# A packed V for quad 3, its transposes inside the next K, and four masks on GpSimd

## The chip, the cores and the metric

The kernel runs on one core of one Trainium2 chip. The metric is the device time of one execution in microseconds (us). Before the change it is 3111.47 us, the median of 3 runs (3111.46 to 3111.81).

## What is computed

A sequence of 2048 positions with 640 channels goes through four layers, A, B, A, B, each behind a layer norm and added to its input. Layer A cuts the sequence into 64 segments of 32 positions. Each segment is put behind 8 memory rows, so that 40 rows attend to each other in 32 heads of 192 channels, and its first 8 output rows are the memory of the next segment. Layer B is a sliding window: each position attends to 8 positions at a distance of 0, 2, ... 14, in 32 heads of 20 channels.

```python
# layer A, one segment: h = [mem; xs], 8 + 32 rows
scores = jnp.einsum('bhqe,bhke->bhqk', q, k) * scale
scores = jnp.where(mask[None, None], scores, -1000000000.0)
p = _softmax(scores, axis=-1)
o = jnp.einsum('bhqk,bhke->bhqe', p, v)
o = jnp.einsum('bhte,hed->btd', o, Wo)
mem = o[:, :M, :].copy()
...
x = x + _A_ref(_layernorm(x, axis=-1), A_mem0, A_Wq, A_Wk, A_Wv, A_Wo, A_seg_len)
x = x + _B_ref(_layernorm(x, axis=-1), B_wqkv, B_wo)
x = x + _A_ref(_layernorm(x, axis=-1), A_mem0, A_Wq, A_Wk, A_Wv, A_Wo, A_seg_len)
x = x + _B_ref(_layernorm(x, axis=-1), B_wqkv, B_wo)
```

## The kernel before, in words

**Lanes and steps.** The two A layers share their weights, and so do the two B layers. The kernel therefore works on two segments at once, called lanes: lane 0 is segment t of the first pair of layers, lane 1 is segment t - 2 of the second pair. A step t does layer A for both lanes (80 columns, NT, of 2 x 40 rows) and, threaded through it, layer B of the step before (64 columns). There are 66 such steps and a last one for layer B alone; 62 of the 66 have both lanes. `one_lane()` is true in the first two and the last two, and what is said below of packing holds for the 62 others.

**Quads.** The 32 heads of layer A are worked in 8 quads of four, numbered 0 to 7. For quad i TensorE computes K (`a_k`), Q (`a_q`) and V (`a_v`), 30 matmuls of 80 columns each, by `proj` (L286); then the scores (`a_s`, 8 matmuls), and, one quad later, the product of probabilities and V (`a_pv`, 8 matmuls). The output projection (`a_o`) of quad i - 5 is put between. The order on every engine is the order in which the program issues the instructions: `run` (L974) puts TensorE, ScalarE, VectorE, GpSimd and SyncE under a manual schedule. `step` (L865) writes that order out by hand. For quad i it is: K of i; the transposes of V of quad i - 1, if that is not packed; Q of i; a piece of layer B (`b_first`); `a_pv` of quad i - 1; V of i; another piece of layer B (`b_second`); the normalisation of quad i - 1 (`a_norm`); the scores of i and their exponential; the mask.

**V and its transposes.** V comes out of TensorE with its channels on the partitions; `a_pv` needs the keys there. `a_v` (L336) copies it to SBUF (tile vT), TensorE transposes it into PSUM (tile ps_vt), and copies bring it into the tile Vt. Without packing (`a_vt`, L354) there are 6 transposes of 128 columns and one VectorE copy (L363). With packing (`a_vt_packed`, `a_vt_main`, `a_vt_rest`), quads 1, 5 and 6 so far, the 80 key rows of two head pairs are laid into 4 transposes: 64 rows of one head pair and the other's fill the 128 rows of three of them, and the 16 left of each share the fourth. That fourth one is copied to the tile Vx (L372) and from there into Vt with six small copies (L387 to L389, three for each head pair), and VectorE copies the rest in two pieces (L380). In quads 5 and 6 GpSimd makes three of the small copies and ScalarE the other three.

**Softmax.** ScalarE makes E, the exponential of the scores (L403). The mask is a product of E with zeros and ones (`a_mask`, L410 for a packed quad, L413 for the others), on VectorE but for quad 5, where GpSimd makes it. The sum over keys comes from columns of ones in Vt. After `a_pv`, ScalarE turns the sums into reciprocals (tile R: four logarithms, L429, and one exponential, L431), and VectorE multiplies (`a_norm`, L439 to L441).

**Layer B.** Its pieces lie at: quad 1, its Q and K; quads 1 to 3, the expansion of its queries on GpSimd (`b_qexp`, L607, five of them, tile QX with two buffers); quads 2 and 3, its scores in four groups (`b_s`, L622, groups 0 and 2 ahead of `a_pv`, 1 and 3 behind `a_s`), their exponentials on ScalarE (tile EB, L628) and masks on VectorE (`b_mask`, L635); quad 3, five transposes of its V (`b_vt`, L596) and two copies of them (tile VB, L600); quad 5, its products (`b_pv`).

The weights come by DMA from the SyncE queue. `used` frees a slot of the weight ring and `prefetch` issues the next load.

Of the kernel before, what the change touches and what calls it, by code (L numbers as in the profile page):

```python
# [13 lines left out]
ALU = mybir.AluOpType  # L14
# [3 lines left out]
P = 128  # L18
# [8 lines left out]
NT = 2 * LT  # L27
# [7 lines left out]
BG = 8  # L35
# [11 lines left out]
MM = 5  # L47
VH = 512
PK = P - NT
PACKED = (1, 5, 6)  # L50

def half_order():

# [27 lines left out]
class Kernel:  # L81
# [201 lines left out]

        return self.acc[int(c >= 3)], c - 3 * int(c >= 3)

    def proj(self, kind, i, t):  # L286

        nc = self.nc
        hT = self.hT
        ps = self.big(f"ps_{kind}", {"k": 0, "q": 1, "v": 2}[kind])  # L290
        w = [self.units[kind, i, h] for h in range(2)]
        mem_last = kind == "k" and i == 0
        order = [(n, c) for c in range(NC) for n in range(6)] if mem_last else [(n, c) for n in range(6) for c in range(NC)]
        for n, c in order:
            if n == 3 and c == 0 and not mem_last:
                self.used(kind, i, (0,))
            nc.tensor.matmul(ps[:, NT * n + self.c0:NT * n + self.c1], lhsT=w[n // 3][:, c, P * (n % 3):P * (n % 3 + 1)],  # L297
                             rhs=hT[:, NT * c + self.c0:NT * c + self.c1],
                             start=(c == 0 and (n == 0 or not mem_last)), stop=(c == NC - 1), skip_group_check=mem_last)
        self.used(kind, i, (0, 1) if mem_last else (1,))  # L300
        return ps

    def a_k(self, i, t):
        nc = self.nc
        ps = self.proj("k", i, t)
        pv = self.cols(ps[:, 0:6 * NT].rearrange("p (a b n) -> p a b n", a=2, b=3))
        h4 = lambda tl: self.cols(tl[:, 0:4 * NT].rearrange("p (a j n) -> p a j n", a=2, j=2))
        kf, kz = h4(self.KF), h4(self.Kz)
        nc.scalar.copy(out=kf, in_=pv[:, :, 0:3:2, :])  # L309
        nc.scalar.copy(out=kz[0:64, :, 0, :], in_=pv[0:64, :, 1, :])  # L310
        nc.scalar.copy(out=kz[64:P, :, 1, :], in_=pv[64:P, :, 1, :])
# [38 lines left out]
    def packed(self, i):  # L350

        return i in PACKED and not self.one_lane()

# [21 lines left out]
    def a_vt_main(self):  # L375
# [3 lines left out]
        for a in range(2):  # L379
            self.nc.vector.tensor_copy(out=dst[64 * a:64 * (a + 1), a], in_=src[64 * a:64 * (a + 1)])  # L380

    def a_vt_rest(self, a, copy):

        halves = lambda v: v.rearrange("p (b c) -> p b c", b=2)
        r0, n = ((64, 16), (32, 32))[a]
        row = self.Vt[r0:r0 + n, VH * a:VH * (a + 1)]
        copy(out=row[:, 0:128], in_=self.Vx[0:n])  # L387
        copy(out=halves(row[:, 128:384])[:, :, 0:64], in_=halves(self.Vx[32:32 + n]))
        copy(out=row[:, 320:448], in_=self.Vx[64:64 + n])  # L389
# [13 lines left out]
        nc.scalar.activation(out=self.cols(e[0:self.rows]), in_=self.cols(sv[0:self.rows]), func=ACT.Exp, scale=float(DH) ** -0.5)  # L403
        self.em = e

    def a_mask(self, eng=None):
        nc, e = self.nc, self.em
        n = self.c1 - self.c0
        if self.rows == P:
            (eng or nc.vector).tensor_tensor(out=e[:].rearrange("p (a j) n -> p a j n", a=2), in0=e[:].rearrange("p (a j) n -> p a j n", a=2),  # L410
                                    in1=self.maskA[:].unsqueeze(2).to_broadcast([P, 2, 2, NT]), op=ALU.mult)
            return
        nc.vector.tensor_tensor(out=self.cols(e[0:NT]), in0=self.cols(e[0:NT]),  # L413
                                in1=self.cols(self.maskA[0:NT, 0]).unsqueeze(1).to_broadcast([NT, 4, n]), op=ALU.mult)

    def a_pv(self):
# [214 lines left out]
    def b_mask(self, b, g):  # L631
        e = self.ebs[g]
        mask = self.maskB[b % 2]
        n = self.on.stop - self.on.start
        self.nc.vector.tensor_tensor(out=e[:, :, self.on], in0=e[:, :, self.on], in1=mask[:, self.on].unsqueeze(1).to_broadcast([P, BG, n]), op=ALU.mult)  # L635

    def b_pv(self, g):

# [87 lines left out]
    def b_first(self, b, i):  # L726

        if i == 2:
            self.b_v(b)
        if i == 4:  # L730
            self.b_mask(b, 3)
        if i == 5:
            self.b_pv(0)
            self.b_norm(0)
        if i == 6 and not self.one_lane():
            self.b_ot()
        if i == 3 and self.one_lane():
            self.b_vt()
        if 2 <= i <= 3:
            self.b_s(2 * i - 4)  # L740
        if i == 3 and not self.one_lane():
            self.b_vt()
        if 2 <= i <= 3:
            self.b_mask(b, 2 * i - 4)

# [117 lines left out]
    def step(self, t):  # L863
        T = self.n_seg + LAG
        nc = self.nc  # L865
        self.set_lanes(t)
        b = t - 1 if t >= 1 else None
        nt = t + 1
        if t == T:
            return self.b_alone(b)  # L870
        for i in range(NQUAD - 1):
            self.a_k(i, t)
            if b is not None and i == 6 and self.one_lane():
                self.b_norm(1)
            if i >= 1 and not self.packed(i - 1):
                self.a_vt(i - 1)
            if b is not None and i == 1:
                self.b_ln_apply(b)
            if b is not None and i == 3:
                self.b_mask(b, 1)  # L880
            self.a_q(i, t)
            if b is not None and i == 0:
                self.bterms = self.ln_terms(self.nc.vector, self.bsums)
            if b is not None:
                self.b_first(b, i)
            if i >= 1:
                self.a_pv()
            if b is not None and i == 6 and self.one_lane():
                self.b_ot()
            self.a_v(i, t)  # L890
            if b is not None:
                self.b_second(b, i)
            if i >= OLAG:
                self.a_o(i - OLAG)
            if b is not None and i == 5:
                self.b_pv(1)
            if i >= 1:
                self.a_norm(i - 1)
            self.a_s(i)
            if b is not None and i == 0:  # L900
                self.b_ln(b)
            if self.packed(i):
                self.a_vt_packed(i)
                if i == 5:
                    self.a_mask(nc.gpsimd)
                self.a_vt_rest(1, nc.gpsimd.tensor_copy)
                if i > 1:
                    self.a_vt_rest(0, nc.scalar.copy)
                if b is not None and i == 5:
                    self.b_norm(1)  # L910
                self.a_vt_main()
                if i == 1:
                    self.a_vt_rest(0, nc.vector.tensor_copy)
            if not (self.packed(i) and i == 5):
                self.a_mask()
            if b is not None and i == 0:
                self.b_ln_rstd()
            if b is not None and 2 <= i <= 3:
                self.b_s(2 * i - 3)
            if b is not None and i == 6:  # L920
                self.b_wo(b)
            if b in (0, LAG) and i == 6:
                self.band_block(self.maskB[0], 1, 0, int(b == LAG))
            if i == 1:
                if nt < self.n_seg:
                    self.x_load(nt)
                yseg = t - 2 - LAG
                if yseg >= 0 and yseg % 2 == 1:
                    self.y_store(yseg // 2)
        self.a_k(7, t)  # L930
        if not self.packed(6):
            self.a_vt(6)
        self.a_q(7, t)
        if nt < T:
            self.ln1_sums(nt)
        self.a_pv()
        self.a_v(7, t)
        self.a_o(7 - OLAG)
        self.a_norm(6)
        self.a_s(7)  # L940
        self.a_vt(7)
        self.a_mask()
        self.a_o(8 - OLAG)
        self.a_o(9 - OLAG, slice(0, NC), False)
        if nt < T:
            self.ln1(nt)
        self.a_pv()
        if nt < T:
            self.ln1_rstd()
        self.a_norm(7)  # L950
        self.a_o(9 - OLAG, slice(NC, None))
        for i in range(10 - OLAG, 7):
            if t == 0:
                self.warm(16)
            self.a_o(i)
        if nt < T:
            self.ln1_apply(nt)
        if t == 0:
            order = [(m, c) for m in (0, 2, 1) for c in range(NC)] + [(m, c) for cs in ((0, 1, 2), (3, 4)) for m in (3, 5, 4) for c in cs]
            self.warm(8)  # L960
            self.a_o(7, slice(0, 3 * NC), False, order)
            self.warm(16)
            self.a_o(7, slice(3 * NC, None), True, order)
        else:
            self.a_o(7)
        if nt < T:
            self.mem_out(t)
        self.b_x1(t)
# [78 lines left out]
```

## Time and profile before

| What | Value |
|---|---|
| median of 3 runs | 3111.47 us (3111.46 to 3111.81) |
| time of the profiled execution | 3109.04 us |
| span of the profile, first to last instruction | 3107.3 us |
| TensorE busy with matmuls | 3056.4 us, 98% |
| VectorE busy | 2437.6 us, 78% |
| ScalarE busy | 1957.8 us, 63% |
| GpSimd busy | 770.1 us, 25% |
| granted TensorE clock, mean | 0.994 |

A name of a group is the tile that is written and the line of the program. In the timeline a row gives the start, the length, the engine, the line, and in square brackets how long the engine had been idle and what released it. Matmuls follow each other in a pipeline: a row of x30 with a length of 1.24 us is followed 1.07 us after its start by the next row. The steps with two lanes repeat every 46.4 us; the step that begins at 1524.3 us is used as the example.

### The profile page before, as it was taken

The page shows a single profiled execution, that of the slowest core. Times are in us where ns is not written, and L with a number is a line of the kernel's source. Part 1 is how long each engine was busy: PE and PEld are TensorE (multiplying, and loading weights), DVE is VectorE, ACT ScalarE, POOL GpSimd, SP SyncE. Part 2 cuts the span into 40 slices and gives each one's busy share as a digit, 9 for nine tenths or more (in the row PEclk, how much of TensorE's full clock was granted, in tenths as well). Part 3 has the DMA queues.
Part 4 walks back from the last instruction along what each step waited for, and adds up shares of the span by engine and source line. Part 5 has one row for each costly group of instructions (what it writes and reads, how often), then busy time and mean ns, then how long its engine had stood idle before and what let it go on. Part 6 is the DMA issues. An engine that isn't in the chain of part 4 may idle for free.

```text
span 3107.3 us, 188174 instructions
## 1 busy us (share of the span) xinstructions
PE 3056.4 (98%) x83082; PEld 3008.0 (97%) x83082; DVE 2437.6 (78%) x6691; ACT 1957.8 (63%) x5984; POOL 770.1 (25%) x1650
## 2 busy tenths in 40 slices
PE   6999999999999999999999999999999999999998
PEld 4899999999999999999999999999999999999997
DVE  3677877878887878877878877878877877878876
ACT  2566666666666666666666666666666666666664
POOL 2122222222222222222222222222222222222221
PEclk7999999999999999999999999999999999999999
DMA  9877777777777777777777777777777777777776
GB/s 393 293 240 250 251 247 247 250 242 252 250 248 250 249 246 252 246 248 249 249 247 250 251 245 249 250 249 251 251 244 249 251 247 250 252 243 252 251 252 220
DMA packets 452980, 785.09 MB, mean 253 GB/s; under 512 B 58560, under 2 KB 444352, under 8 KB 452160
## 3 DMA queue, kind: packets, MB, share of 16 engines
q1 hardware_dynamic: 438480, 767.84, 76.2%
q8 instruction: 650, 10.65, 1.4%
q10 hardware_dynamic: 13680, 5.21, 0.7%
q14 instruction: 170, 1.39, 0.1%
HBM read 770.22 MB, written 2.62 MB: 249 GB/s over the span
## 4 chain that ended last, share of the span: by engine, by line
PE 95%; DMA 3%; issue 1%; ACT 0%; POOL 0%; DVE 0%; SPq 0%; ACTq 0%; POOLq 0%; DVEq 0%
PE ps_acc L456 18%; PE ps_k L297 17%; PE ps_q L297 17%; PE ps_v L297 17%; PE ps_o L425 5%; PE ps_vt L362 3%; PE ps_s L400 2%; PE ps_s L401 2%; PE ps_bs L622 2%; PE ps_bk L570 2%; PE ps_bq L570 1%; PE ps_bv L570 1%; PE ps_by L681 1%; PE ps_vt L371 1%; PE ps_vr L331 1%
## 5 line engine op out<-in xcount | busy, mean ns | idle before, releaser
L429 ACT ACTIVATE R<-ps_o 64x160 f32<-64x160 f32 (+1 forms) x2112 | 622.0, 295 | 317.9 <-PE ps_o L425 153.8
L297 PEld LDWEIGHTS <-w_ring 128*128 128x128 bf16 x16470 | 675.4, 100 | 17.8 <-issue 4.2
L607 POOL TENSOR_TENSOR QX<-QB,hmask 128x448 bf16<-128x448 bf16 (+2 forms) x325 | 304.9, 947 | 1206.0 <-ACT QB L585 963.6
L297 PE MATMUL ps_q<-hT,w_q 128*128 128x80 bf16 (+1 forms) x12870 | 541.2, 201 | 5.7 <-DMA w_q<-in_A_Wq_dram 4.6
L297 PEld LDWEIGHTS <-w_q 128*128 128x128 bf16 x12870 | 492.5, 100 | 7.1 <-DMA w_q<-in_A_Wq_dram 5.6
L456 PE MATMUL ps_acc<-OT,w_o 128*128 128x80 bf16 (+1 forms) x9900 | 458.3, 200 | 4.0 <-DMA w_o<-in_A_Wo_dram 2.1
L297 PE MATMUL ps_v<-hT,w_v 128*128 128x80 bf16 (+1 forms) x9480 | 422.8, 202 | 2.1 <-DMA w_v<-in_A_Wv_dram 1.4
L316 DVE CAST QT<-ps_q 128x480 bf16<-128x480 f32 (+1 forms) x528 | 337.2, 639 | 92.2 <-PE ps_q L297 87.3
L309 ACT CAST KF<-ps_k 128x320 bf16<-128x320 f32 (+1 forms) x528 | 219.0, 415 | 297.7 <-PE ps_k L297 288.7
L456 PEld LDWEIGHTS <-w_o 128*128 128x128 bf16 x9900 | 392.7, 100 | 5.2 <-DMA w_o<-in_A_Wo_dram 2.9
L403 ACT ACTIVATE E<-ps_s 80x320 bf16<-80x320 f32 (+2 forms) x528 | 222.1, 421 | 243.7 <-PE ps_s L401 236.8
L297 PE MATMUL ps_k<-hT,w_k 128*128 128x80 bf16 (+1 forms) x7920 | 372.4, 201 | 3.0 <-DMA w_k<-in_A_Wk_dram 2.3
L297 PEld LDWEIGHTS <-w_v 128*128 128x128 bf16 x9480 | 371.1, 100 | 2.6 <-DMA w_v<-in_A_Wv_dram 1.5
L297 PE MATMUL ps_k<-hT,w_ring 128*128 128x80 bf16 (+1 forms) x7860 | 370.6, 201 | 2.5 <-DMA w_ring<-in_A_Wk_dram 1.5
L439 DVE TENSOR_TENSOR OT<-ps_o,R 128x320 bf16<-128x320 f32 (+1 forms) x528 | 254.0, 481 | 131.3 <-ACT R L431 114.3
L297 PEld LDWEIGHTS <-w_k 128*128 128x128 bf16 x7920 | 322.0, 100 | 3.7 <-DMA w_k<-in_A_Wk_dram 2.6
L456 PE MATMUL ps_acc<-OT,w_ring 128*128 128x80 bf16 (+1 forms) x5940 | 307.7, 201 | 1.4 <-DMA w_ring<-in_A_Wo_dram 1.1
L348 DVE CAST vT<-ps_v 128x480 bf16<-128x480 f32 (+1 forms) x318 | 206.9, 651 | 83.3 <-PE ps_v L297 76.3
L297 PE MATMUL ps_v<-hT,w_ring 128*128 128x80 bf16 (+1 forms) x5640 | 264.8, 202 | 2.7 <-issue 2.2
L431 ACT ACTIVATE R<-R 128x320 f32<-128x320 f32 (+1 forms) x528 | 243.8, 462 | 16.6
L456 PEld LDWEIGHTS <-w_ring 128*128 128x128 bf16 x5940 | 248.7, 100 | 3.7 <-DMA w_ring<-in_A_Wo_dram 1.3
L425 PE MATMUL ps_o<-E,Vt 80*128 80x80 bf16 (+2 forms) x4224 | 236.8, 200 | 0.8 <-DVE Vt L363 0.5
(171 smaller groups left out, 5439.6 us busy)
## 6 DMA issues: line engine op xcount, KB each, us to landing
w_ring<-in_A_Wk_dram SPq DMA_DIRECT2D x1036, 240.0 KB, 3.7
w_ring<-in_A_Wo_dram SPq DMA_DIRECT2D x780, 240.0 KB, 3.7
w_ring<-in_A_Wv_dram SPq DMA_DIRECT2D x776, 240.0 KB, 3.9
w_ring<-in_A_Wq_dram SPq DMA_DIRECT2D x390, 240.0 KB, 3.8
w_q<-in_A_Wq_dram SPq DMA_DIRECT2D x5, 960.0 KB, 11.2
w_v<-in_A_Wv_dram SPq DMA_DIRECT2D x6, 480.0 KB, 11.3
w_ring<-in_A_Wk_dram SPq DMA_DIRECT2D x6, 480.0 KB, 10.5
w_ring<-in_A_Wo_dram SPq DMA_DIRECT2D x6, 480.0 KB, 11.3
```

The costliest lines, as they stand in the source:

```text
L297: nc.tensor.matmul(ps[:, NT * n + self.c0:NT * n + self.c1], lhsT=w[n // 3][:, c, P * (n % 3):P * (n % 3 + 1)], rhs=hT[:, NT * c + self.c0 ...
L309: nc.scalar.copy(out=kf, in_=pv[:, :, 0:3:2, :])
L316: self.nc.vector.tensor_copy(out=self.cols(qt[:]), in_=self.cols(ps[:, 0:6 * NT].rearrange("p (a n) -> p a n", a=6)))
L348: nc.vector.tensor_copy(out=self.cols(self.vT[:, 0:6 * NT].rearrange("p (a n) -> p a n", a=6)), in_=self.cols(ps[:, 0:6 * NT].rearrange("p ...
L403: nc.scalar.activation(out=self.cols(e[0:self.rows]), in_=self.cols(sv[0:self.rows]), func=ACT.Exp, scale=float(DH) ** -0.5)
L425: nc.tensor.matmul(self.cols(ov[:, pr, k]), lhsT=vt[0:self.rows, VH * pr + c0:VH * pr + c0 + P], rhs=self.cols(em[0:self.rows, 2 * pr + k ...
L429: nc.scalar.activation(out=self.cols(r[r0:r0 + 64, :, j]), in_=self.cols(src), func=ACT.Ln)
L431: nc.scalar.activation(out=rf, in_=rf, func=ACT.Exp, scale=-1.0)
L439: nc.vector.tensor_tensor(out=oc[:, :, 0:3:2], in0=ov[:, :, 0:4:3], in1=r, op=ALU.mult)
L456: nc.tensor.matmul(self.cols(acc[:, k]), lhsT=w[m // 3][:, m % 3, P * c:P * (c + 1)], rhs=self.cols(ot[:, m]), start=(i == 0 and m == 0 an ...
L570: nc.tensor.matmul(ps[:, NX * n + self.on.start:NX * n + self.on.stop], lhsT=self.wqkv[:, part, c, P * n:P * (n + 1)], rhs=self.h2T[:, c, ...
L607: self.nc.gpsimd.tensor_tensor(out=qx[:, 0:nh, self.on], in0=self.qb[:, c, self.on].unsqueeze(1).to_broadcast([P, nh, n]), in1=self.hmask[ ...
```

## The change

V of quad 3 is packed, as that of quads 1, 5 and 6. Its four transposes are not issued behind the scores of quad 3 but in the middle of K of quad 4, between its 15th and 16th matmul, where `proj` now calls a function that it is given. The copy to Vx and the six small copies are issued there as well; so those on ScalarE stand ahead of ScalarE's copies of K of quad 4. The two large copies (`a_vt_main`) are issued behind K of quad 4.

The five transposes of layer B's V, with their two copies, go from quad 3 to quad 4, where they stand ahead of `a_pv` of quad 3.

The masks of quads 2, 3 and 4, and that of layer B's last group of scores, go from VectorE to GpSimd. That of quad 5 was there and stays. In the steps with one lane all stay as they were.

```diff
-PACKED = (1, 5, 6)
+PACKED = (1, 3, 5, 6)
+POOL_MASK = (2, 3, 4, 5)
...
-    def proj(self, kind, i, t):
+    def proj(self, kind, i, t, between=None):
...
             if n == 3 and c == 0 and not mem_last:
                 self.used(kind, i, (0,))
+                if between is not None:
+                    between()
...
+    def a_vt_early(self, i):
+
+        self.a_vt_packed(i)
+        self.a_vt_rest(1, self.nc.gpsimd.tensor_copy)
+        if i > 1:
+            self.a_vt_rest(0, self.nc.scalar.copy)
...
-    def a_mask(self, eng=None):
+    def a_mask(self, i):
         nc, e = self.nc, self.em
+        eng = nc.gpsimd if i in POOL_MASK and not self.one_lane() else nc.vector
...
+        eng = self.nc.gpsimd if g == 3 and not self.one_lane() else self.nc.vector
+        eng.tensor_tensor(out=e[:, :, self.on], in0=e[:, :, self.on], in1=mask[:, self.on].unsqueeze(1).to_broadcast([P, BG, n]), op=ALU.mult)
...
         if i == 4:
+            if not self.one_lane():
+                self.b_vt()
             self.b_mask(b, 3)
...
-        if i == 3 and not self.one_lane():
-            self.b_vt()
...
-            self.a_k(i, t)
+            mid = i == 4 and self.packed(3)
+            self.a_k(i, t, (lambda: self.a_vt_early(3)) if mid else None)
+            if mid:
+                self.a_vt_main()
...
+            if i in POOL_MASK:
+                self.a_mask(i)
+            if self.packed(i) and i != 3:
+                self.a_vt_early(i)
...
-            if not (self.packed(i) and i == 5):
-                self.a_mask()
+            if i not in POOL_MASK:
+                self.a_mask(i)
```

More of the change, by code (lines that the diff above doesn't have):

```diff
@@ L301, in proj, with a_k @@
         return ps
-    def a_k(self, i, t):
+    def a_k(self, i, t, between=None):
         nc = self.nc
-        ps = self.proj("k", i, t)
+        ps = self.proj("k", i, t, between)
         pv = self.cols(ps[:, 0:6 * NT].rearrange("p (a b n) -> p a b n", a=2, b=3))
@@ L404, in a_s @@
         self.em = e
-    def a_mask(self, eng=None):
+    def a_mask(self, i):
         nc, e = self.nc, self.em
+        eng = nc.gpsimd if i in POOL_MASK and not self.one_lane() else nc.vector
         n = self.c1 - self.c0
         if self.rows == P:
-            (eng or nc.vector).tensor_tensor(out=e[:].rearrange("p (a j) n -> p a j n", a=2), in0=e[:].rearrange("p (a j) n -> p a j n", a=2),
+            eng.tensor_tensor(out=e[:].rearrange("p (a j) n -> p a j n", a=2), in0=e[:].rearrange("p (a j) n -> p a j n", a=2),
                                     in1=self.maskA[:].unsqueeze(2).to_broadcast([P, 2, 2, NT]), op=ALU.mult)
             return
-        nc.vector.tensor_tensor(out=self.cols(e[0:NT]), in0=self.cols(e[0:NT]),
+        eng.tensor_tensor(out=self.cols(e[0:NT]), in0=self.cols(e[0:NT]),
                                 in1=self.cols(self.maskA[0:NT, 0]).unsqueeze(1).to_broadcast([NT, 4, n]), op=ALU.mult)
@@ L634, in b_mask @@
         n = self.on.stop - self.on.start
-        self.nc.vector.tensor_tensor(out=e[:, :, self.on], in0=e[:, :, self.on], in1=mask[:, self.on].unsqueeze(1).to_broadcast([P, BG, n]), op=ALU.mult)
+        eng = self.nc.gpsimd if g == 3 and not self.one_lane() else self.nc.vector
+        eng.tensor_tensor(out=e[:, :, self.on], in0=e[:, :, self.on], in1=mask[:, self.on].unsqueeze(1).to_broadcast([P, BG, n]), op=ALU.mult)
     def b_pv(self, g):
@@ L901, in step @@
                 self.b_ln(b)
[L902 to L908, printed above, removed]
+            if i in POOL_MASK:
+                self.a_mask(i)
+            if self.packed(i) and i != 3:
+                self.a_vt_early(i)
                 if b is not None and i == 5:
@@ L941, in step @@
         self.a_vt(7)
-        self.a_mask()
+        self.a_mask(7)
         self.a_o(8 - OLAG)
```

## The prediction, as made before the run

> **What bounds the kernel now.** I read the page's shares of busy time first, and its chain of the work that ended last.
>
> ```profile
> PE 3056.4 (98%) x83082; PEld 3008.0 (97%) x83082; DVE 2437.6 (78%) x6691; ACT 1957.8 (63%) x5984; POOL 770.1 (25%) x1650
> ...
> PE 95%; DMA 3%; issue 1%; ACT 0%; POOL 0%; DVE 0%; SPq 0%; ACTq 0%; POOLq 0%; DVEq 0%
> ```
>
> TensorE is busy 98% and carries the chain. Of the waits by engine, TensorE's own list is a few us in all, mostly in the first and last steps; for Vt it waits 0.5 us in the whole run. So every instruction taken from TensorE saves its spacing, unless a new wait appears, and every wait of TensorE is lost. The question is how near the waits are. For that I read the timeline of one step with both lanes, first of TensorE (start, length), in quads 3 to 5:
>
> ```profile
> 1541.26 0.41 PE L622 MATMUL ps_bs<-QX,KB 128*128 128x256 bf16 x2
> 1541.50 0.44 PE L596 MATMUL ps_bvt<-ident,VTB 128*128 128x128 bf16 x5
> 1541.78 0.45 PE L425 MATMUL ps_o<-E,Vt 80*128 80x80 bf16 x8
> ...
> 1544.75 0.50 PE L362 MATMUL ps_vt<-ident,vT 128*128 128x128 bf16 x6
> 1545.09 1.24 PE L297 MATMUL ps_q<-hT,w_q 128*128 128x80 bf16 x30
> 1546.16 0.45 PE L425 MATMUL ps_o<-E,Vt 80*128 80x80 bf16 x8
> ```
>
> The first L425 row is `a_pv` of quad 2, the second that of quad 3. Then ScalarE:
>
> ```profile
> 1541.70 0.60 ACT L628 ACTIVATE EB<-ps_bs 128x512 bf16<-128x512 f32 x1 [0.59 <-PE ps_bs L622]
> 1542.33 1.23 ACT L429 ACTIVATE R<-ps_o 64x160 f32<-64x160 f32 x4
> 1543.59 0.47 ACT L431 ACTIVATE R<-R 128x320 f32<-128x320 f32 x1
> ...
> 1544.96 0.43 ACT L309 CAST KF<-ps_k 128x320 bf16<-128x320 f32 x1
> ...
> 1546.70 1.23 ACT L429 ACTIVATE R<-ps_o 64x160 f32<-64x160 f32 x4 [0.84 <-ACT Kz L311]
> ```
>
> and VectorE:
>
> ```profile
> 1544.82 0.33 DVE L441 TENSOR_TENSOR OT<-ps_o,R 64x160 bf16<-64x160 f32 x1
> 1545.18 0.32 DVE L413 TENSOR_TENSOR E<-E,maskA 80x320 bf16<-80x320 bf16 x1
> 1545.53 0.55 DVE L363 COPY Vt<-ps_vt 80x768 bf16<-80x768 bf16 x1
> ...
> 1549.55 0.32 DVE L413 TENSOR_TENSOR E<-E,maskA 80x320 bf16<-80x320 bf16 x1
> 1549.91 0.56 DVE L363 COPY Vt<-ps_vt 80x768 bf16<-80x768 bf16 x1
> ```
>
> Read together they are one chain: layer B's group 2 ends on TensorE, ScalarE makes its exponential (1541.70), only then R of quad 2 (to 1544.06), VectorE normalises (to 1545.15), masks, and copies Vt of quad 3, to 1546.08. The weight load of `a_pv` starts 0.05 later, at 1546.13, and TensorE gets there at 1546.16. There is no slack to give. The same holds one quad on: Vt of quad 4 is there at 1550.47, `a_pv` of quad 4 starts at 1550.52.
>
> **What goes from TensorE.** Two of six transposes. Six take 0.34 us from start to start (1544.75 to 1545.09), so 0.056 each, 0.112 per step; over 62 steps 6.9 us. The Trainium skill, "TensorE: Matmul & The Clock Gate", Part 4, gives about 275 ns for a transpose of this size inside a kernel; by it the two would be worth 34 us (estimate). The trace does not agree as far as spacing goes: their own length is 0.220, the spacing 0.056.
>
> **The first new wait: `a_pv` of quad 3.** The five transposes of layer B (0.28) go from ahead of `a_pv` of quad 2 to ahead of that of quad 3, so TensorE comes to the latter at 1546.16 - 0.11 = 1546.05. What must be ready: E, and Vt. The chain up to the normalisation does not move: R waits for the exponential of group 2 on ScalarE, not for `a_pv`, which now ends 0.28 sooner. So Vx, queued behind the normalisation on VectorE, starts at 1545.18, where the mask stood; its transposes, near 1543.94 to 1544.34, are long done. For what follows Vx, quad 6 is the template, where nothing else holds the copies up. VectorE there:
>
> ```profile
> 1513.11 0.33 DVE L441 TENSOR_TENSOR OT<-ps_o,R 64x160 bf16<-64x160 f32 x1
> 1513.47 0.22 DVE L372 COPY Vx<-ps_vt 96x128 bf16<-96x128 bf16 x1
> ```
>
> and ScalarE:
>
> ```profile
> 1513.72 0.29 ACT L387 COPY Vt<-Vx 16x128 bf16<-16x128 bf16 x1 [0.68 <-DVE Vx L372]
> 1514.04 0.30 ACT L388 COPY Vt<-Vx 16x128 bf16<-16x128 bf16 x1
> 1514.36 0.29 ACT L389 COPY Vt<-Vx 16x128 bf16<-16x128 bf16 x1
> 1514.68 0.43 ACT L309 CAST KF<-ps_k 128x320 bf16<-128x320 f32 x1
> ```
>
> So from the start of Vx the third ScalarE copy ends 1.18 later, VectorE's two large ones 0.87 later, GpSimd's third 1.26 (1.37 where it took 0.40). Here: ScalarE 1546.36, VectorE 1546.05, GpSimd 1546.44. The weight loads do not all wait for all of it: in the trace of quad 5 each of the first, second and fourth load of a half waits for its own small copy. With 0.05 from a copy's end to the load, the fourth load starts at 1546.41 instead of 1546.16. Four loads more, 0.036 apart, and V of quad 4 starts at 1546.59 instead of 1546.45: **0.14 per step later than before**, saving included (0.19 if GpSimd's third copy takes 0.40; I take 0.29, for 0.40 was beside a VectorE mask).
>
> **The second: `a_pv` of quad 4.** The three ScalarE copies stand ahead of KF and Kz of quad 4 and wait for Vx. As in quad 6, KF starts 0.32 behind the third copy, 1546.39 instead of 1544.96, and Kz ends at 1547.30. The scores of quad 4 (near 1547.67) still find it. But R of quad 3 then starts at 1547.31 instead of 1546.70, 0.61 late. VectorE's normalisation is late by as much, and so is Vt of quad 4, less the mask that leaves VectorE between the two (0.36 from L413 to L363): 0.25. Vt is there at 1550.71, the load at 1550.76; TensorE comes at 1550.52 + 0.14 = 1550.66. From such a late load to the next projection takes 0.30 (1457.77 to 1458.07, one of the few times it happens now), against 0.29. So V of quad 5 starts at 1551.06 instead of 1550.81: **0.245 per step in all**. It swallows the first wait, and the saved transposes with it: the end is set by ScalarE and VectorE. Quad 5 then has an output projection ahead of its products, and quads 5 and 6 only shift.
>
> **What I cost at nothing, and its cover.** Masks on GpSimd: the same product of 128x320 takes 0.79 there and 0.38 on VectorE; the form of 80x320 isn't in the trace on GpSimd, bounds 0.32 (VectorE) and 0.95 (QX of 128x448), I take 0.79. Quad 2: E and QX both end at 1539.84, masked 1540.7, needed 1541.50. Quad 3: 1544.46 to 1545.25, needed 1546.05, and 0.2 ahead of GpSimd's copies. Quad 4: E is 0.61 late, 1549.45 to 1550.24, needed 1550.66. Each cover is 0.4 or more; each 0.1 beyond it would cost 6.2 us. Layer B's last mask (QX of 128x512: 1.04) runs near 1546.5 to 1547.6, ahead of quad 4's mask, and is needed in quad 5. The Trainium skill, "GPSIMD Engine Reference", section 4.1, puts two-input elementwise work at about twice VectorE's time and advises against it; the trace agrees (0.79 to 0.38). If the path took it, 3 x 0.41 x 62 = 76 us.
>
> The casts of V of quad 3 (0.56 and 0.25, second next to start 0.72 on, for 0.66) end near 1543.79, since V now ends 0.28 sooner; the transposes in K come at 1543.94. If they were late, TensorE would wait in K, but up to 0.25 of that is lost at `a_pv` anyway. Layer B's two copies (0.55) fall behind Q of quad 4, where VectorE then has nothing until V. Nothing is moved past a DMA: the inserted function is called after the ring's release and issues none.
>
> **Sum.** 62 x 0.245 = 15.2 us. On the profiled execution (3109.04, its span 3107.3) 3124.2; the median lies 2.4 above it, so **3126.7 us**, 0.49% slower.
>
> **Rivals.**
> - *Only the first wait* (0.15): R of quad 3 is less late than I say, and Vt of quad 4 is in time. 62 x 0.14 to 0.19 = 8.7 to 11.8 us: 3120 to 3123. For it: the second needs three shifts in a row to carry over. Against: ScalarE's order fixes them.
> - *Coarser waits* (0.08): all loads of `a_pv` wait for the last small copy, GpSimd's at 0.40: load at 1546.60, V at 1546.90, 0.45 late, and no second wait. 3139 (3133 at 0.29). Against: quad 5's loads start at 1509.57, GpSimd's last copy ends at 1509.62.
> - *No wait, faster* (0.08): Vx does not stand behind the normalisation, because R of quad 2 comes sooner now that `a_pv` does. Then the 6.9 us stay: 3104.5. It decides if R ends 0.36 us sooner (0.245 + 0.112), at 1543.70; ScalarE's exponential of group 2 would have to be off its way. Only 0.28 is freed on TensorE. If transposes cost TensorE their 0.220, this would be 3084; I give that 0.01 of the 0.08.
> - *Masks bind* (0.04): GpSimd takes 0.5 us longer than its rows, with VectorE beside it. Quad 3's mask then pushes GpSimd's copies by 0.3 (the mask led them by 0.2), its eighth load starts at 1546.79 instead of 1546.55, V is 0.38 late: 3135.
> - *Half of it* (0.05): waits of less than 0.1, within 0.2%.
>
> The rest, 0.60, is the forecast, with 3124 to 3130 of its own. About 0.2% (6.2 us) is what a measurement of this kernel can tell from no change. Slower 0.60 + 0.15 + 0.08 + 0.04 = 0.87, same 0.05, faster 0.08. The range takes in the forecast, the first rival, and the low end of the second: 3116 to 3134.
>
> **What would show it.** In the changed profile: the transposes of L362 fall by 6 x 62 and those of L371 rise by 4 x 62. TensorE's waits at `ps_o` L425 appear, for ScalarE's or GpSimd's Vt in quad 3 (some 0.25 per step) and for VectorE's Vt in quad 4 (0.1). KF of quad 4 starts 1.4 us later in the step, R of quad 3 0.6 later. GpSimd's masks end 0.4 us or more ahead of `a_pv`. I am wrong if Vx starts before the normalisation has ended, or if a wait appears at K or Q.

## The result, and the profile after

The changed kernel takes 3126.01 us (median of 6 runs, 3122.70 to 3127.86), against 3111.64 us (6 runs, 3111.26 to 3112.62) for the kernel before. The ratio is 1.0045, with a 95% interval of 1.0032 to 1.0058: 14.4 us slower. 3126.7 us was predicted.

The page of the changed kernel, its busy shares and its chain:

```profile
PE 3070.9 (98%) x82958; PEld 3012.2 (96%) x82958; DVE 2399.0 (77%) x6629; ACT 2006.4 (64%) x6170; POOL 1036.9 (33%) x2084
...
PE 86%; ACT 6%; DMA 3%; DVE 3%; issue 1%; POOL 0%; SPq 0%; ACTq 0%; POOLq 0%; DVEq 0%
```

TensorE has 124 matmuls fewer (2 x 62) and is "busy" 14.5 us longer. That is how a short wait looks on this page: each matmul counts as busy for its own 0.2 us, though the next one usually starts 0.036 us after it, so a wait of less than 0.2 us leaves no idle time. The chain says it more plainly: ScalarE and VectorE, at 0% before, now hold 9% of it.

TensorE's weight loads by what they waited for (total us, times, longest):

```profile
PEld L436 <- ACT Vt L399: 12.4, 61, 0.2
```

One new row, 61 times: `a_pv` (now L436) waits for ScalarE's third small copy, once per step, for 0.20 where some 0.25 was forecast. The second wait, of 0.1 by the forecast, for VectorE's Vt of quad 4, is hardly in the list: loads of `a_pv` that wait for VectorE's Vt appear twice, with 0.4 us in all. It must be read from the timeline. From here on times are counted from "the zero" of a step, the start of ScalarE's exponential of layer B's group 2, where the prediction's chain begins. This is TensorE, in a step whose zero is at 1548.30 (1541.70 in the step shown of before):

```profile
1552.37 0.45 PE L607 MATMUL ps_bvt<-ident,VTB 128*128 128x128 bf16 x5
1552.65 0.76 PE L436 MATMUL ps_o<-E,Vt 128*128 128x80 bf16 x8
1553.25 0.70 PE L300 MATMUL ps_v<-hT,w_v 128*128 128x80 bf16 x15
...
1557.09 0.36 PE L660 MATMUL ps_bo<-VB,EB 128*128 128x41 bf16 x8
1557.37 0.46 PE L436 MATMUL ps_o<-E,Vt 80*128 80x80 bf16 x8
```

`a_pv` of quad 3 starts 4.35 behind the zero, 0.11 sooner than before, and then takes 0.60 to the next projection instead of 0.29: it stops in its middle. `a_pv` of quad 4 starts 0.28 behind the eight products of L660, which need 0.22 (1550.30 to 1550.52 in the step of before). The weight loads show where the first one stops:

```profile
1552.60 0.21 PEld L436 LDWEIGHTS <-Vt 128*128 128x128 bf16 x3
1553.01 0.27 PEld L436 LDWEIGHTS <-Vt 128*128 128x128 bf16 x5 [0.20 <-ACT Vt L399]
```

Three loads go, the fourth waits until 1553.01, 0.05 behind the end of ScalarE's third copy. ScalarE, and then VectorE:

```profile
1548.30 0.60 ACT L639 ACTIVATE EB<-ps_bs 128x512 bf16<-128x512 f32 x1 [0.60 <-PE ps_bs L633]
...
1552.02 0.29 ACT L397 COPY Vt<-Vx 16x128 bf16<-16x128 bf16 x1 [0.56 <-DVE Vx L375]
...
1552.66 0.29 ACT L399 COPY Vt<-Vx 16x128 bf16<-16x128 bf16 x1
1552.98 0.43 ACT L312 CAST KF<-ps_k 128x320 bf16<-128x320 f32 x1
...
1553.91 1.23 ACT L440 ACTIVATE R<-ps_o 64x160 f32<-64x160 f32 x4
```

```profile
1551.41 0.33 DVE L452 TENSOR_TENSOR OT<-ps_o,R 64x160 bf16<-64x160 f32 x1
1551.77 0.22 DVE L375 COPY Vx<-ps_vt 96x128 bf16<-96x128 bf16 x1
...
1556.76 0.55 DVE L366 COPY Vt<-ps_vt 80x768 bf16<-80x768 bf16 x1
```

Vx follows the normalisation, the small copies follow Vx, and KF (with Kz, ScalarE's copies of K) follows the small copies. R of quad 3 follows KF and Kz (5.61 behind the zero; 5.00 before). Vt of quad 4 ends at 1557.31 and its product starts at 1557.37. The masks on GpSimd are done well before each `a_pv`:

```profile
1551.05 0.79 POOL L421 TENSOR_TENSOR E<-E,maskA 128x320 bf16<-128x320 bf16 x1 [1.84 <-ACT E L413]
...
1556.04 0.79 POOL L424 TENSOR_TENSOR E<-E,maskA 80x320 bf16<-80x320 bf16 x1 [1.71 <-ACT E L413]
```

Over 60 steps the medians are steady to some nanoseconds. In the table, V of quad 4 and of quad 5 are the first matmul behind each `a_pv`, in us from the zero. The columns after them set 62 times the lateness of V of quad 5 beside what was measured against the kernel before in the same series.

| Kernel | V of quad 4 | V of quad 5 | 62 x late, us | measured, us | ratio, 95% interval |
|---|---|---|---|---|---|
| before | 4.748 | 9.108 | | | |
| changed | 4.950 | 9.362 | +15.7 | +14.4 | 1.0045 (1.0032 to 1.0058) |
| e1, not packed | 4.748 | 9.086 | -1.4 | -1.6 | 0.9995 (0.9986 to 1.0004) |
| e2, packed only | 5.311 | 10.080 | +60.3 | +56.1 | 1.0178 (1.0158 to 1.0198) |
| e3, mask of quad 4 on VectorE | 4.950 | 9.715 | +37.6 | +35.6 | 1.0112 (1.0092 to 1.0132) |
| e4, more work for TensorE | 4.954 | 9.372 | +16.4 | +13.2 | 1.0042 (1.0028 to 1.0057) |
| e5, Vx two products sooner | 4.669 | 9.009 | -6.1 | -6.2 | 0.9982 (0.9974 to 0.9991) |
| e6, KF first | 5.228 | 9.562 | +28.1 | +28.3 | 1.0090 (1.0072 to 1.0107) |

In the rest of the step nothing moves: from V of quad 5 to the next zero the changed kernel's timeline is the old one, 0.25 late. The two profiled executions differ by more, 18.8 us of span; the changed kernel's is the longest of its six runs, and some steps are longer at irregular places (by over 0.1 us in 29 of 61, and in 22 of 61 before), behind waits named "issue" or a weight's DMA. What causes those was not tried.

### The profile page after: what moved, and what is told of

Same layout as the page of the kernel before. It is cut to its first block, busy times and chain, and to the rows that moved or that the text cites. A ratio compares the mean times of both kernels' runs of the same rounds, so it can differ in the third digit from the quotient of the medians.

```text
span 3126.1 us, 188608 instructions
## 1 busy us (share of the span) xinstructions
PE 3070.9 (98%) x82958; PEld 3012.2 (96%) x82958; DVE 2399.0 (77%) x6629; ACT 2006.4 (64%) x6170; POOL 1036.9 (33%) x2084
## 4 chain that ended last, share of the span: by engine, by line
PE 86%; ACT 6%; DMA 3%; DVE 3%; issue 1%; POOL 0%; SPq 0%; ACTq 0%; POOLq 0%; DVEq 0%
PE ps_acc L467 17%; PE ps_k L300 15%; PE ps_q L300 15%; PE ps_v L300 15%; PE ps_o L436 5%; PE ps_vt L365 3%; ACT R L440 2%; PE ps_s L410 2%; PE ps_s L411 2%; PE ps_bs L633 2%; PE ps_bk L581 2%; PE ps_bv L581 2%; PE ps_bq L581 1%; PE ps_by L693 1%; PE ps_vt L374 1%
## 5 line engine op out<-in xcount | busy, mean ns | idle before, releaser
L300 PE MATMUL ps_k<-hT,w_ring 128*128 128x80 bf16 (+1 forms) x7860 | 380.7, 201 | 4.0 <-DMA w_ring<-in_A_Wk_dram 2.2
L436 PE MATMUL ps_o<-E,Vt 128*128 128x80 bf16 (+2 forms) x4224 | 251.5, 200 | 4.4
L351 DVE CAST vT<-ps_v 128x480 bf16<-128x480 f32 (+1 forms) x256 | 166.0, 649 | 97.6 <-PE ps_v L300 97.6
```

The costliest lines, as they stand in the source:

```text
L351: nc.vector.tensor_copy(out=self.cols(self.vT[:, 0:6 * NT].rearrange("p (a n) -> p a n", a=6)), in_=self.cols(ps[:, 0:6 * NT].rearrange("p ...
L436: nc.tensor.matmul(self.cols(ov[:, pr, k]), lhsT=vt[0:self.rows, VH * pr + c0:VH * pr + c0 + P], rhs=self.cols(em[0:self.rows, 2 * pr + k ...
```

## The experiments

All are the changed kernel with one edit. e1 to e4 ran on a chip where the kernel before took 3104.81 us, e5 and e6 where it took 3106.31 us, so only ratios and differences within a series are compared.

**e1: the masks and the moved transposes without the packing.**

```diff
-PACKED = (1, 3, 5, 6)
+PACKED = (1, 5, 6)
```

> The changed kernel with quad 3 unpacked again; its masks stay on GpSimd and layer B's transposes stay one quad on. Chain theory (ScalarE's three small copies of Vt of quad 3, behind the normalisation, hold up first a_pv of quad 3 and then, by way of KF, Kz and R, that of quad 4): without the copies Vt of quad 3 follows the normalisation directly, 0.36 us sooner than before the change, nothing is late, and no instruction leaves TensorE: 3111.6 us, within 0.1% of the kernel before. Rival (the masks on GpSimd at 0.79 us, or the moved transposes, cost the time): a part or all of the 14.4 us stays, 3118 to 3126 us.

3103.22 us, ratio 0.9995: no difference that this measurement can tell. VectorE, in e1:

```profile
1545.31 0.33 DVE L452 TENSOR_TENSOR OT<-ps_o,R 64x160 bf16<-64x160 f32 x1
1545.67 0.55 DVE L366 COPY Vt<-ps_vt 80x768 bf16<-80x768 bf16 x1
```

Vt of quad 3 now follows the normalisation where the mask stood, and VectorE is idle for 0.36 behind it. Without the packing, masks on GpSimd and the moved transposes cost nothing that shows: the loss belongs to the packing of quad 3. V of quad 5 even comes 0.02 sooner: `a_pv` of quad 4 had waited that much for Vt before the change.

**e2: the packing without the masks and the moved transposes.**

```diff
-POOL_MASK = (2, 3, 4, 5)
+POOL_MASK = (5,)
...
-        eng = self.nc.gpsimd if g == 3 and not self.one_lane() else self.nc.vector
+        eng = self.nc.vector
...
         if i == 4:
-            if not self.one_lane():
-                self.b_vt()
             self.b_mask(b, 3)
...
             self.b_s(2 * i - 4)
+        if i == 3 and not self.one_lane():
+            self.b_vt()
```

> The changed kernel with the masks of quads 2 to 4 and of layer B's last group on VectorE again and layer B's transposes back in quad 3; only the packing of quad 3 stays. Chain theory: the mask of quad 3 stands between the normalisation and Vx again (0.41 us), so ScalarE's copies, KF, Kz and R of quad 3 come 0.41 us later than in the changed kernel, 1.02 us later than before; the mask of quad 4 stands ahead of Vt of quad 4 again (0.36 us). a_pv of quad 4 is then about 1.02 us late per step: 62 x 1.02 = 63 us, 3175 us. Rival (only the first wait, at a_pv of quad 3, counts): about 0.60 us per step, 3149 us. Rival (the masks cost the time): faster than the changed kernel, near 3105 us.

3160.86 us, ratio 1.0178. The rival of the first wait alone (3149 on the old scale, ratio 1.012) lies below the interval; so does that of the masks. The forecast of 63 us was 7 too high: 3 of them because the mask of quad 3 took less than its mean, the other 4 lie between the lateness in the trace (60.3) and the measured 56.1. VectorE, in e2:

```profile
1570.17 0.33 DVE L421 TENSOR_TENSOR E<-E,maskA 128x320 bf16<-128x320 bf16 x1
1570.53 0.22 DVE L375 COPY Vx<-ps_vt 96x128 bf16<-96x128 bf16 x1
```

From mask to Vx it is 0.36, not 0.41, and R of quad 3 starts at 5.97 behind the zero, not 6.02. So the masks on GpSimd, with the moved transposes, were worth some 42 us to a kernel with quad 3 packed (56.1 less 14.4), and nothing to one without (e1).

**e3: the mask of quad 4 alone back on VectorE.**

```diff
-POOL_MASK = (2, 3, 4, 5)
+POOL_MASK = (2, 3, 5)
```

> The changed kernel with the mask of quad 4 alone back on VectorE. Chain theory: it stands between the normalisation of quad 3 and Vt of quad 4, which comes 0.36 us later, and a_pv of quad 4 with it; that wait is the one that sets the end, so 62 x (0.25 + 0.36) = 38 us over the kernel before, 3149 us. Rival (the wait at a_pv of quad 3 sets the loss of 0.20 us per step, and quad 4 has slack): quad 4 becomes late by less than 0.36, at most 0.05 at a time for the trace of after, 3126 to 3129 us. Rival (the mask on GpSimd is itself the cost): faster than the changed kernel.

3140.45 us, ratio 1.0112, 35.6 us: the mask's place on VectorE (0.35 from V of quad 5's column) comes out at the end in full. V of quad 4 is where it is in the changed kernel, so the first wait is the same and the second sets the step. Weight loads by what they waited for, in e3:

```profile
PEld L436 <- DVE Vt L366: 22.7, 62, 0.4
...
PEld L436 <- ACT Vt L399: 12.5, 61, 0.2
```

Now that the second wait is longer than a matmul's tail, the list shows it, beside the first.

**e4: five transposes more, ahead of `a_pv` of quad 3.**

```diff
-        for n in range(NC):
+        for n in list(range(NC)) * (1 if self.one_lane() else 2):
             nc.tensor.transpose(out=ps[:, n, :], in_=self.VTB[:, n, :], identity=self.ident[:])
```

> The changed kernel with layer B's five transposes of each two-lane step issued twice, directly ahead of a_pv of quad 3: 0.28 us more of TensorE work per step that changes no result. Chain theory: ScalarE and VectorE set the time from layer B's group 2 to a_pv of quad 4, TensorE has 0.36 us to spare there (0.25 lost and 0.11 saved), so nothing changes: 3126 us, within 2 us of the changed kernel, and by the same token the two transposes that the change took from TensorE earned nothing. Rival (TensorE is the bound there as elsewhere, each instruction counts): 62 x 0.28 = 17.4 us more, 3143 us.

3118.01 us, ratio 1.0042 (1.0028 to 1.0057), beside 1.0045 for the changed kernel; 17.4 us more would have been 1.010. TensorE, in e4, in a step whose zero is 1544.24:

```profile
1548.31 0.72 PE L607 MATMUL ps_bvt<-ident,VTB 128*128 128x128 bf16 x10
1548.87 0.49 PE L436 MATMUL ps_o<-E,Vt 128*128 128x80 bf16 x8
1549.20 0.70 PE L300 MATMUL ps_v<-hT,w_v 128*128 128x80 bf16 x15
```

`a_pv` starts 4.63 behind the zero instead of 4.35, hardly stops any more (0.33 to the next projection; 0.29 without a wait), and V of quad 4 comes at 4.95 as before the edit. From group 2 of layer B to `a_pv` of quad 4 the changed kernel is not bound by TensorE, and 0.28 us of matmuls ahead of `a_pv` of quad 3 fit in free of charge. So the two transposes saved there were worth nothing either.

**e5: Vx ahead of two of the three products of the normalisation.**

```diff
     def a_vt_early(self, i):

         self.a_vt_packed(i)
+        if i == 3:
+            self.a_norm(2, (1,))
         self.a_vt_rest(1, self.nc.gpsimd.tensor_copy)
...
-                self.a_norm(i - 1)
+                self.a_norm(i - 1, (0,) if i == 3 and self.packed(3) else (0, 1))
```

`a_norm` gets a second argument here: (0,) makes the first product alone, (1,) the other two.

> The changed kernel with one reordering on VectorE: of the three products that normalise quad 2, the first keeps its place and the other two are issued behind the copy to Vx of quad 3, so that the six small copies need not wait for them (0.64 us). Chain theory, in us from the start of ScalarE's exponential of layer B's group 2: the first product starts at 2.39, Vx at 2.80 instead of 3.47; ScalarE's copies 3.19 to 4.12 (from its exponential of group 3 on), Kz ends at 5.07, R of quad 3 starts at 5.08 (5.61 in the changed kernel, 5.00 before), Vt of quad 4 is in time; VectorE's large copies end near 4.4, GpSimd's third near 4.56, by which the eighth load is up to 0.05 late. Both waits go, and what stays is the saving: 62 x (0.05 - 0.11), 3.7 us under the kernel before, ratio 0.9988, between 0.9978 (no wait at all) and 1.0000. Rival (TensorE waits for something else of the packing, the masks or the insertion into K): the ratio stays at 1.003 or more.

3100.12 us, ratio 0.9982 (0.9974 to 0.9991): faster than both kernels, by 6.2 us on its chip. VectorE, ScalarE and TensorE, in e5, in a step whose zero is 1538.32:

```profile
1540.70 0.49 DVE L455 TENSOR_TENSOR OT<-ps_o,R 128x320 bf16<-128x320 f32 x1 [0.29 <-ACT R L444]
1541.11 0.21 DVE L375 COPY Vx<-ps_vt 96x128 bf16<-96x128 bf16 x1
```

```profile
1541.51 0.30 ACT L399 COPY Vt<-Vx 16x128 bf16<-16x128 bf16 x1
...
1543.39 0.61 ACT L442 ACTIVATE R<-ps_o 64x160 f32<-64x160 f32 x2
```

```profile
1542.67 0.49 PE L438 MATMUL ps_o<-E,Vt 128*128 128x80 bf16 x8
1542.99 0.71 PE L300 MATMUL ps_v<-hT,w_v 128*128 128x80 bf16 x15
```

Vx starts 2.79 behind the zero, R of quad 3 at 5.07. `a_pv` of quad 3 takes 0.32 to the next projection instead of 0.60: 0.03 more than without any wait, which fits GpSimd's third copy (it ends at 1542.90). V of quad 4 is 0.08 sooner than before the change and V of quad 5 0.10; the forecast had 0.06, for it took the eighth load to be 0.05 late, and left out the 0.02 that `a_pv` of quad 4 had waited before. The masks, the packing and the insertion into K are all as in the changed kernel; where Vx stands on VectorE decides the sign.

**e6: KF and Kz ahead of ScalarE's small copies.**

```diff
-        if i > 1:
+        if i > 3:
             self.a_vt_rest(0, self.nc.scalar.copy)
...
             if mid:
+                self.a_vt_rest(0, nc.scalar.copy)
                 self.a_vt_main()
```

> The changed kernel with ScalarE's three small copies of quad 3 issued behind its copies KF and Kz of quad 4 instead of ahead of them. Chain theory: KF starts at 3.19 us from the exponential of layer B's group 2 (4.68 in the changed kernel), the small copies run from 4.11 to 5.05, and the wait moves from a_pv of quad 4 to that of quad 3: its fourth load at 5.10 instead of 4.71, V of quad 4 at 5.34, 0.59 later than before the change; R of quad 3 then starts near 5.6, as in the changed kernel, and quad 4 adds nothing. 62 x 0.59 = 37 us over the kernel before, ratio 1.0118. Rival (the delay of KF and R is the whole loss, and the small copies have slack): ratio 1.000 or under.

3134.59 us, ratio 1.0090. The wait does move to `a_pv` of quad 3, but V of quad 4 is 0.48 us late, not 0.59, and the ratio lies below the 1.0118 that was expected. ScalarE, in e6, zero at 1555.19:

```profile
1558.39 0.42 ACT L312 CAST KF<-ps_k 128x320 bf16<-128x320 f32 x1
...
1559.01 0.29 ACT L314 CAST Kz<-ps_k 64x160 bf16<-64x160 f32 x1
1559.20 0.29 ACT L397 COPY Vt<-Vx 16x128 bf16<-16x128 bf16 x1
...
1559.83 0.29 ACT L399 COPY Vt<-Vx 16x128 bf16<-16x128 bf16 x1
```

The first small copy starts 0.19 behind the start of the last Kz, where I had reckoned 0.30, and all follows 0.11 sooner. The rival that the small copies have slack is out. Neither order of the two on ScalarE is good while Vx comes so late.

## Why the prediction was right

**The bound and the knife edge.** Right. TensorE was the bound, for e1 gives VectorE 0.36 back in the chain and gains only 0.02 a step. The chain from group 2's exponential to Vt had no slack either, for those 0.02 were a wait for Vt of quad 4 that was already there (the load at 8.809 behind the zero, 0.053 behind the end of Vt; at 8.780 in e1).

**The saving.** The two transposes take 0.112: `a_pv` of quad 3 arrives at 4.350 instead of 4.460. e5 shows that most of it can be kept: V of quad 5 is 0.10 sooner there, 0.08 of the saving and the 0.02 that quad 4 had waited. By the 275 ns for a transpose of the Trainium skill, "TensorE: Matmul & The Clock Gate", Part 4, e5 should have gained far more (estimate: 0.55 a step). The measured spacing, 0.056, decides.

**The first wait.** Right in place and cause, and mis-sized: V of quad 4 comes 0.20 late, not 0.14. The fourth load starts when it was forecast, 4.71 behind the zero. Two things behind it were counted too short. The fifth load starts 0.072 behind the fourth instead of 0.036: the trace has a wait instruction of its own there, for VectorE's large copies. They had ended at 1552.64, but it runs from 1553.00 to 1553.05, only once the fourth load has been released; in e5, where the fourth load isn't late, the distance is 0.035. And from the fourth load to V takes 0.21 without any wait (4.539 to 4.748 before), where the prediction allowed 0.18; its 1546.16 for the fourth load of before is the start of the first product, and the fourth load was at 1546.24. The coarser rival, all loads at the last copy, is out: three loads start 0.3 to 0.4 ahead of the fourth.

**The second wait.** Right, and it sets the step: 0.254 a step against 0.245, R of quad 3 at 5.61 as forecast. That it swallows the error of the first is luck: a first wait longer by 0.1 would have set the step itself. e3 isolates it (0.35 more on VectorE in this place, 0.35 more a step), and e4 shows from the other side that TensorE has time ahead of it. The time alone does not tell it from the rival of the first wait alone. With the 4.334 that e6 takes from V of quad 4 to V of quad 5, where quad 4 adds nothing, the first wait would make V of quad 5 0.18 late and cost 11 us (an estimate), and the measured interval goes from 10 to 18 us. The trace does tell it: V of quad 5 is 0.254 late.

**What was costed at nothing.** Right: e1. GpSimd's mask of 80x320 takes 0.79, as does the one of 128x320. Layer B's took 1.15 instead of 1.04 and nothing waited for it. The Trainium skill, "GPSIMD Engine Reference", section 4.1, would rather have masks on VectorE; per instruction the trace agrees (0.79 against 0.33). Per kernel VectorE's 0.33 stood in the chain and GpSimd's 0.79 did not: with quad 3 packed, moving the mask of quad 4 alone is worth 21 us (e3 against the changed kernel, 35.6 less 14.4).

**The sum.** 15.2 us forecast, 62 x 0.254 = 15.7 by the trace, 14.4 measured. That the forecast ends within 0.7 us of the median is partly luck: the same way of reckoning missed by 7 us in e2 and by 9 in e6. Why e2 to e4 were measured 2 to 4 us below their lateness is not shown. The lateness could take up irregular waits of TensorE inside the stretch, but over 61 steps of the trace of before they come to only 0.9 us. Outside the stretch the steps of e2 to e4 are in sum some 5 us shorter than those of before, whose profile comes from another series, so that settles nothing.

**The faster rival.** It was said to decide if R ended 0.36 sooner. What decided in e5 was not R, but what stands between R and Vx. The rival had the right condition, that Vx must not stand behind the normalisation, and named only one way to it.

## What to carry to other kernels

An instruction taken from the busiest engine earns its spacing only where that engine is what the end waits for; here the stretch of 9 us behind one exponential was ScalarE's and VectorE's, and 0.28 us of matmuls could be added there free. Splitting one copy into a chain of small ones over other engines must be counted from the instruction that it is queued behind, and for what is queued behind it: the three small copies delay their own product by 0.20, and through KF and R, which have nothing to do with them, the next quad's by 0.25. Before moving work between engines, try the order on the engine at the head of the chain: one copy moved ahead of two products turned 0.45% lost into 0.18% gained.

## What was not expected of the hardware

A weight load that has waited is followed more slowly than usual (0.072 instead of 0.036) when a separate wait instruction stands behind it, even one whose copies had ended 0.36 us earlier; where the load is not late, the same instruction costs nothing that shows (0.035 in e5). Small ScalarE copies of 16x128 follow each other at 0.32 us, no faster than the 64x160 casts at 0.30: three of them take 0.93, longer than the one VectorE copy of 80x768 (0.55) that they help to replace.
